# Order of the first chunks, the first weights and the crossbar transposes in a fused retention and Swish kernel

## The chip, the cores and the metric

The kernel runs on one core of one Trainium2 chip. The metric is the device time of one execution in microseconds; the median over several runs counts. A profile is of one single execution and has its own time.

## The reference, cut to what matters

```python
B, H, S, D = 8, 8, 576, 64                     # q, k, v: float32 [B, H, S, D]
scores = (1 / sqrt(D)) * (q @ k.transpose(0, 1, 3, 2))
gamma = 1 - 2 ** (-5 - arange(H))
Dmat = where(i >= j, gamma[h] ** (i - j), 0)   # causal decay, positions i and j
att = (scores * Dmat) @ v
x = att.transpose(0, 2, 1, 3).reshape(B * S, H * D)     # 4608 x 512
h = x @ w_in                                   # 512 x 2048
g = h * sigmoid(beta * h)                      # beta: one number for each of the 2048 columns
out = g @ w_out                                # 2048 x 512, float32
```

## The kernel before, in words

The decay is split into a factor of the query's position (`gq`, with the scale) and one of the key's position (`gv`, put on the values). What is left of the decay within a chunk is a mask of ones and zeros. The first 512 positions of each batch element are four **chunks** of 128; the last 64 positions of two batch elements together make a **tail** of 128 rows. In the list `seq` (lines 51 to 56) the chunks and tails are numbered in the order in which they are attended: 0 to 3 are batch 0, 4 to 7 batch 1, 8 to 11 batch 2, 12 to 15 batch 3, 16 the first tail, 17 to 20 batch 4, 21 a tail, 22 to 25 batch 5, 26 to 29 batch 6, 30 a tail, 31 to 34 batch 7, 35 the last tail. A state (keys by values, summed in PSUM) carries what a chunk hands on to the next.

A chunk's steps are these functions. `load_kv` (line 84) loads its keys and values on SyncE's queue in rows of 64 numbers (256 bytes). `pre` (248) scales and casts them on POOL into `kn` and `vn`. The keys are then transposed, for chunks 0 to 7 on TensorE through PSUM (`t_k`, 293), and later for two chunks at once by a crossbar DMA that ScalarE issues (`x_k`, 279, through `turn`, 273). The queries have the same two ways: `load_q`, `pre_q` (234), `t_q` (286) or `x_q` (276); a tail has `load_tail` and `x_tail` (283). `a_sc` (306) makes the scores in two PSUM tiles and masks them on VectorE into `R`; `a_st` (367) adds to the state, which ScalarE copies to SBUF; `a_cross` (321) is the part of the output that comes from the state; `a_O` (341) is the part within the chunk, and copies the transposed result into `xT`, the input of the second half.

The second half works on **blocks** of 512 rows (the four chunks of a batch element; block 8 holds the tails). `up` (387) multiplies by 128 columns of `w_in` in four matmuls, and ScalarE applies Swish from PSUM into `gT` (396); it can be given a part of the chunks (`c0`, `cn`). `down` (400) multiplies by four of the sixteen row groups of `w_out` and, at the last of them, copies the sum on VectorE into `ot` (414) and stores it from SyncE. Both use the PSUM tag `mm` with three buffers. The weights come as float32 pieces (`pieces`, 159; `load_w_in`, `load_w_out`) into four staging buffers, which the output also uses, and are cast to bf16 (`cast_w_in`, 173; `cast_w_out`, 187).

The order of the work is written by hand, and every engine runs its instructions in that order. Lines 438 to 466 are the start: queries of block 0, chunks 0, 1, 2, the first weights. From line 474 a list `fill` holds the calls of `up` and `down` in order, and `streams` holds the other steps, each with a number. `merged` (424) puts a step ahead of the fill item whose index is not below its number. `d0` is the index of block 0's first `down`, `u1` that of block 1's first `up`. Block 0's up is split: four products for chunks 0 to 2, then four for chunk 3 alone, then twelve whole ones; chunk 3 is attended among them (`steps(3, ...)`). From block 2 on, `group` (505) sets the steps of each chunk at distances ahead of the place `at` of its scores. `load_kv` has six buffers, `load_q` two, `kn` and its transpose three pairs, `vn` five. A SyncE load that waits for a buffer holds up what is queued behind it, and a crossbar transpose that ScalarE issues stands between its activations.

## Time and profile before

| what | value |
|---|---|
| median of 13 runs | 322.5 us (320.68 to 325.67) |
| the profiled execution: its time | 321.35 us |
| its span, first to last instruction | 319.6 us |
| TensorE matmuls busy | 302.5 us (95%) |
| ScalarE busy | 138.4 us |
| VectorE busy | 108.0 us |
| POOL busy | 96.0 us |
| moved by DMA | 53.82 MB |
| first up product of block 0 | 17.47 us |
| first down product of block 0 | 35.49 us |
| first up product of block 1 | 58.10 us |
| scores of chunk 8 (block 2) | 70.48 us |
| first up product of block 2 | 94.18 us |

All times within the execution count from the start of the span. A line of the timeline gives start, duration, engine, line, operation, what is written from what, the shape and the count; in brackets is the idle time of that engine just before and what ended it. PE is TensorE, ACT is ScalarE, DVE is VectorE, SPq and ACTq are the queues on which SyncE and ScalarE issue DMAs. Matmuls overlap, so the busy time of TensorE is more than its work.

### The profile page before, as it was taken

What the parts mean: (1) busy time and instruction counts of PE and PEld (TensorE: products, weight loads), DVE (VectorE), ACT (ScalarE), POOL (GpSimd) and SP (SyncE); (2) the same over time, 40 slices, a digit from 0 to 9 for tenths busy, and PEclk for the clock granted to TensorE, in tenths of its full rate; (3) what the DMA queues carried; (4) which work ended last, traced back from release to release, by engine and by line L of the source; (5) the groups of instructions that cost most, each with busy time, mean ns of one, the idle gap of its engine ahead of it and who ended that gap; (6) DMA issues with size and microseconds to landing.
All of it is one profiled execution on the core that took longest, in us unless ns stands there. A gap on an engine that the chain in (4) does not pass through costs nothing.

```text
span 319.6 us, 5205 instructions
## 1 busy us (share of the span) xinstructions
PE 302.5 (95%) x2078; PEld 153.0 (48%) x2113; DVE 108.0 (34%) x191; ACT 138.4 (43%) x241; POOL 96.0 (30%) x127
## 2 busy tenths in 40 slices
PE   7779988979999999999999999999799999999996
PEld 5545445434554445444444444444345444444444
DVE  6746456113560135224423343234324420010012
ACT  5567726654127601770067206720275117406700
POOL 2652075834530562174227120292220000000000
PEclk9799999999999999999999999999999999999999
DMA  8999999999979969995999736969841110032012
GB/s 208 259 345 386 372 208 269 248 207 204 229 198 157 238 139 225 231 198 128 229 246 157 161 102 129 250 102 225 215 39 33 68 66 0 2 79 53 2 59 72
DMA packets 127591, 53.82 MB, mean 168 GB/s; under 512 B 109888, under 2 KB 119504, under 8 KB 127568
## 3 DMA queue, kind: packets, MB, share of 16 engines
q1 hardware_dynamic: 97968, 46.15, 61.3%
q10 hardware_dynamic: 29600, 7.35, 14.5%
q8 instruction: 16, 0.26, 0.4%
q14 instruction: 7, 0.06, 0.1%
HBM read 36.71 MB, written 9.44 MB: 144 GB/s over the span
## 4 chain that ended last, share of the span: by engine, by line
PE 74%; DMA 13%; SPq 5%; POOL 3%; issue 2%; ACT 1%; DVE 1%; ACTq 0%; POOLq 0%; DVEq 0%
PE po L407 33%; PE ph L394 31%; DMA kT<-kn 9%; PE O L352 3%; PE sc L314 3%; SPq L91 2%; DMA kvn<-in_k_dram 2%; DMA wt<-in_moe_w_in_dram 2%; PE O L338 2%; PE st L377 2%; SPq L102 1%; SPq L80 1%; POOL qs L244 1%; ACT gT L396 1%; POOL kn L267 1%
## 5 line engine op out<-in xcount | busy, mean ns | idle before, releaser
L394 PE MATMUL ph<-xT,w_in_sb 128*128 128x512 bf16 (+2 forms) x577 | 127.6, 373 | 4.4 <-ACT gT L396 1.6
L407 PE MATMUL po<-w_out_sb,gT 128*128 128x512 bf16 (+2 forms) x588 | 126.6, 367 | 1.2 <-issue 0.3
L396 ACT ACTIVATE gT<-ph,beta_sb 128x512 bf16<-128x512 f32 (+2 forms) x148 | 98.8, 678 | 65.9 <-PE ph L394 64.7
L394 PEld LDWEIGHTS <-w_in_sb 128*128 128x128 bf16 x592 | 56.3, 98 | 68.0 <-issue 3.6
L407 PEld LDWEIGHTS <-gT 128*128 128x128 bf16 x608 | 57.1, 98 | 61.8
L319 DVE TENSOR_TENSOR R<-sc,causal 128x512 bf16<-128x512 f32 x72 | 46.3, 684 | 79.2 <-PE sc L314 79.1
L414 DVE COPY ot<-po 128x512 f32<-128x512 f32 (+2 forms) x38 | 25.2, 663 | 112.3 <-PE po L407 112.3
L244 POOL TENSOR_TENSOR qs<-qn,gq 128x512 bf16<-128x512 f32 x26 | 27.5, 1081 | 66.7 <-DMA qn<-in_q_dram 52.0
L268 POOL TENSOR_TENSOR vn<-kvn,gv 128x512 bf16<-128x512 f32 x32 | 33.3, 1042 | 14.4 <-DMA kvn<-in_v_dram 12.1
L382 ACT CAST sbd<-st 64x256 bf16<-64x256 f32 x48 | 17.6, 367 | 41.9 <-PE st L377 39.0
L267 POOL CAST kn<-kvn 128x512 bf16<-128x512 f32 x32 | 19.5, 609 | 41.8 <-DMA kvn<-in_k_dram 24.6
L382 ACT CAST end<-st 64x256 bf16<-64x256 f32 x16 | 5.9, 367 | 39.5 <-PE st L377 39.4
L365 DVE CAST xT<-O 128x512 bf16<-128x512 f32 x29 | 19.7, 680 | 2.9 <-PE O L352 2.0
L314 PE MATMUL sc<-qT,kT 64*128 64x128 bf16 x256 | 12.9, 221 | 4.9 <-DMA kT<-kn 2.7
L314 PEld LDWEIGHTS <-kT 64*128 64x128 bf16 x288 | 8.2, 95 | 18.6 <-issue 10.8
L352 PE MATMUL O<-R,vn 128*64 128x128 bf16 x288 | 15.3, 227 | 0.0
L377 PE MATMUL st<-vn,kn 128*128 128x128 bf16 x128 | 12.5, 220 | 0.2 <-POOL vn L268 0.2
L352 PEld LDWEIGHTS <-vn 128*64 128x64 bf16 x288 | 9.4, 110 | 4.2 <-issue 0.6
L338 PE MATMUL O<-qT,sbd 128*128 128x128 bf16 x96 | 9.7, 225 | 0.0
L377 PEld LDWEIGHTS <-kn 128*128 128x128 bf16 x128 | 8.5, 99 | 1.3 <-issue 0.2
L204 PE MATMUL ph<-warm 128*128 128x256 f32 (+1 forms) x16 | 6.3, 544 | 1.3 <-DVE warm L113 1.3
L194 DVE TENSOR_SCALAR w_out_sb<-wt,rbeta_sb 128x512 bf16<-128x512 f32 x12 | 5.1, 481 | 5.6 <-DMA wt<-in_moe_w_out_dram 5.6
(55 smaller groups left out, 76.6 us busy)
## 6 DMA issues: line engine op xcount, KB each, us to landing
qn<-in_q_dram SPq DMA_DIRECT2D x16, 512.0 KB, 5.7
kvn<-in_k_dram SPq DMA_DIRECT2D x32, 256.0 KB, 6.3
kvn<-in_v_dram SPq DMA_DIRECT2D x32, 256.0 KB, 5.9
out_dram<-ot SPq DMA_DIRECT2D x31, 256.0 KB, 3.2
wt<-in_moe_w_out_dram SPq DMA_DIRECT2D x4, 1024.0 KB, 9.3
wt<-in_moe_w_in_dram SPq DMA_DIRECT2D x3, 1024.0 KB, 9.6
out_dram<-ot SPq DMA_DIRECT2D x9, 128.0 KB, 2.4
tln<-in_q_dram SPq DMA_DIRECT2D x8, 128.0 KB, 3.8
```

The costliest lines, as they stand in the source:

```text
L244: e.tensor_tensor(batch[b]["qs"][:, cs, hs], q_tiles[b][:, hs, cs].rearrange("p h i d -> p i h d"), gq[:, cs, hs].unsqueeze(3).to_broadcas ...
L267: nc.gpsimd.tensor_copy(kn[:, c % 2], t[:, 0])
L268: nc.gpsimd.tensor_tensor(vn[:], t[:, 1], gains(gv, c), ALU.mult)
L314: nc.tensor.matmul(view(sc[j][:, p, :]), L["kT"][r, p, :], rhs, start=True, stop=True, skip_group_check=True)
L319: nc.vector.tensor_tensor(R[:, j], sc[j][:], m_b, ALU.mult)
L352: nc.tensor.matmul(O[j * D:(j + 1) * D, p, :], vn[:, 2 * p + j, :], R[:, j, p, :], start=p == 0 and not (early and crossed), stop=early or ...
L377: nc.tensor.matmul(st[:, p, :], heads(L["kn"], p), heads(L["vn"], p), start=(c == 0 and p == 0), stop=True, skip_group_check=True)
L382: nc.scalar.copy(s[r, :, j * D:(j + 1) * D], st[r, :, j * D:(j + 1) * D])
L394: nc.tensor.matmul(ph, w_in_sb[:, ko, fo * P:(fo + 1) * P], xts[m][:, ko, :, w], start=(ko == 0), stop=(ko == KO - 1))
L396: nc.scalar.activation(gts[m][:, fo, :, w], ph, ACT.Silu, scale=beta_sb[:, fo:fo + 1])
L407: nc.tensor.matmul(po[:, :nn], gT[:, fo, ms, :], w_out_sb[:, fo, n0:n0 + nn], start=(fo == 0), stop=(fo == FO - 1))
L414: nc.vector.tensor_copy(ot, po[:, :nn])
```

## The change

All four first chunks are loaded ahead of the weights, and chunk 3 is attended in the start like chunks 0 to 2; block 0's up is whole from its first product. The first two pieces of `w_in` become 256 and 256 columns, and their casts go to POOL and VectorE. For chunk 3 ScalarE copies one of the two score tiles to SBUF as bf16 (`half`), and VectorE masks it from there. In block 1, the first four products of up are made for chunks 4 to 6 and then for chunk 7 alone, and chunk 7 is attended among them. The loads of q(2) and of chunks 8 and 9 come right behind those of chunk 7, and chunks 10 and 11 have places of their own. In `group` the loads, the scaling steps and the crossbar transposes have larger distances ahead of the scores.

```diff
-    for n in range(CB - 1):
+    for n in range(CB):
         load_kv(n)
...
-    pieces = [(0, 384), (384, 128)] + [(f, 512) for f in range(512, d_ff, 512)]
+    pieces = [(0, 256), (256, 256)] + [(f, 512) for f in range(512, d_ff, 512)]
...
-    def cast_w_in(g):
-        t = wts.pop(g)
+    def cast_w_in(g, kos=range(KO)):
+        t = wts[g]
         f0, fn = pieces[g]
-        for ko in range(KO):
-            if g == 1 and ko < 2 or g == 0 and ko == 0:
-                nc.scalar.copy(w_in_sb[:, ko, f0:f0 + fn], t[:, ko])
-            else:
-                (nc.gpsimd if g < 2 or ko == KO - 1 else nc.vector).tensor_copy(w_in_sb[:, ko, f0:f0 + fn], t[:, ko])
+        for ko in kos:
+            on_pool = ko == KO - 1 or g == 0 and ko > 0 or g == 1 and ko > 1
+            (nc.gpsimd if on_pool else nc.vector).tensor_copy(w_in_sb[:, ko, f0:f0 + fn], t[:, ko])
...
     for g in range(NP):
-        if g == 1:
-            load_kv(CB - 1)
         load_w_in(g)
...
-        (nc.vector.tensor_copy if i == CB - 1 else nc.scalar.copy)(live[i]["kT"], T[:])
+        nc.scalar.copy(live[i]["kT"], T[:])
...
+        if i == CB - 1:
+
+            half = sb.tile([P, HP, P], BF16, name="half", tag="half", bufs=1)
+            nc.scalar.copy(half[:], sc[1][:])
+            sc[1] = half
         for j in range(2):
             nc.vector.tensor_tensor(R[:, j], sc[j][:], m_b, ALU.mult)
...
-            tag, bufs = ("mm", 3) if i == 1 else ("O", 1)
+            tag, bufs = ("mm", 3) if i in (1, 3) else ("O", 1)
...
-        if i == CB - 2:
+        if i == CB - 1:
             nc.vector.tensor_copy(x[:, :2], O[:, :2])
             nc.scalar.copy(x[:, 2:], O[:, 2:])
         else:
-            (nc.scalar.copy if i < E and i != CB - 1 else nc.vector.tensor_copy)(x, O[:])
+            (nc.scalar.copy if i < E else nc.vector.tensor_copy)(x, O[:])
...
     t_k(2)
     a_st(1)
-    cast_w_in(0)
     a_sc(2)
+    pre(3)
     a_O(1)
     warm_up(1, 128)
     a_cross(2, True)
+    t_k(3)
+    a_st(2)
+    cast_w_in(0, range(1, KO))
+    a_sc(3)
+    a_O(2)
+    a_cross(3, True)
+    a_st(3)
     warm_up(1, 128)
-    a_O(2)
-    a_st(2)
+    cast_w_in(0, range(1))
+    warm_up(1, 128)
+    a_O(3)
+    cast_w_in(1)
...
-    fill = [F(up, 0, fo, 0, CB - 1) for fo in range(4)] + [F(up, 0, fo, CB - 1, 1) for fo in range(4)]
-    fill += [F(up, 0, fo) for fo in range(4, FO)]
+    fill = [F(up, 0, fo) for fo in range(FO)]
     d0 = len(fill)
...
     u1 = len(fill)
-    fill += [F(up, 1, fo) for fo in range(FO)]
+    fill += [F(up, 1, fo, 0, CB - 1) for fo in range(4)] + [F(up, 1, fo, CB - 1, 1) for fo in range(4)]
+    fill += [F(up, 1, fo) for fo in range(4, FO)]
     fill += [F(down, 1, ms, f0) for ms in range(MB // P) for f0 in range(0, FO, 4)]
-    base = {1: u1}
+    base = {1: u1 + 4}
...
-    streams = [steps(3, 0, 1, 2, 3.5, 3.5, 3.5),
-               [(0.1, F(load_w_out, 0)), (2.5, F(cast_w_in, 1)), (6, F(cast_w_in, 2)), (6.2, F(load_w_out, 1)),
-                (10, F(cast_w_in, 3)), (10.1, F(load_w_out, 2)), (14, F(cast_w_in, 4)), (14.1, F(load_w_out, 3))],
-               [(d0 - 4 + 3.5 * g, F(cast_w_out, g)) for g in range(WG)],
-               [(14.2, F(load_q, 1))] + [(14.2, F(load_kv, n)) for n in range(CB, E)],
-               [(d0 + 7, F(pre_q, 1, n)) for n in range(4)] + [(d0 + 8.5, F(t_q, 1, 0)), (d0 + 9.8, F(t_q, 1, 1))],
-               steps(4, d0 + 7.5, d0 + 9.9, d0 + 10.7, d0 + 11.5, d0 + 11.6, d0 + 11.9),
-               steps(5, d0 + 9, d0 + 11.2, d0 + 11.8, d0 + 12.5, d0 + 12.6, d0 + 12.9),
-               steps(6, d0 + 10, d0 + 12.2, d0 + 12.8, d0 + 13.5, d0 + 13.6, d0 + 13.9),
-               steps(7, d0 + 11, d0 + 13.2, d0 + 13.8, d0 + 14.5, d0 + 14.6, d0 + 14.9)]
+    streams = [[(0, F(load_w_out, 0)), (2.1, F(cast_w_in, 2)), (2.2, F(load_w_out, 1)),
+                (6.1, F(cast_w_in, 3)), (6.2, F(load_w_out, 2)), (10.1, F(cast_w_in, 4)), (10.2, F(load_w_out, 3))],
+               [(d0 - 4 + 3.3 * g, F(cast_w_out, g)) for g in range(WG)],
+               [(10.3, F(load_q, 1))] + [(10.3, F(load_kv, n)) for n in range(CB, E)],
+               [(10.4, F(load_q, 2))] + [(10.4, F(load_kv, n)) for n in range(E, E + 2)],
+               [(d0 + 8.6, F(load_kv, E + 2)), (d0 + 10.1, F(load_kv, E + 3))],
+               [(d0 + 8, F(pre_q, 1, n)) for n in range(4)] + [(d0 + 9.6, F(t_q, 1, 0)), (d0 + 10.6, F(t_q, 1, 1))],
+               steps(4, d0 + 8.5, d0 + 11, d0 + 11.8, d0 + 12.7, d0 + 12.8, d0 + 12.9),
+               steps(5, d0 + 10, d0 + 11.9, d0 + 12.8, d0 + 13.7, d0 + 13.8, d0 + 13.9),
+               steps(6, d0 + 11, d0 + 12.95, d0 + 13.8, d0 + 14.7, d0 + 14.8, d0 + 14.9),
+               steps(7, d0 + 12, d0 + 15, u1 + 0.8, u1 + 2.7, u1 + 2.8, u1 + 2.9)]
...
-                st += [(at - 24, F(load_tail, c)), (at - 12, F(pre, i)), (at - 8, F(x_tail, i))]
+                st += [(at - 28, F(load_tail, c)), (at - 14, F(pre, i)), (at - 10, F(x_tail, i))]
...
                 if c == 0:
-                    xs, ps = ((8.5, 7), (14, 13, 12, 11)) if near else ((11, 9.5), (17, 16, 15, 14))
-                    st += [(at - 24, F(load_q, b))] + [(at - a, F(pre_q, b, x)) for x, a in enumerate(ps)]
+                    xs, ps = ((9, 7.5), (14, 13, 12, 11)) if near else ((14, 12.5), (20, 19, 18, 17))
+                    st += [(at - 32, F(load_q, b))] if not near else []
+                    st += [(at - a, F(pre_q, b, x)) for x, a in enumerate(ps)]
                     st += [(at - a, F(x_q, b, x)) for x, a in enumerate(xs)]
                 if c % 2 == 0:
-                    p0, p1, x0 = (13, 12, 8.5) if c else (9, 8.5, 5.5) if near else (13, 12, 7.5)
-                    st += [(at - 23, F(load_kv, n)), (at - 22.5, F(load_kv, n + 1)), (at - p0, F(pre, i)),
-                           (at - p1, F(pre, i + 1)), (at - x0, F(x_k, b, c // 2))]
+                    p0, p1, x0 = (9, 8.5, 6) if near and c == 0 else (16, 15, 10.5)
+                    if not near:
+                        st += [(at - 29, F(load_kv, n)), (at - 26, F(load_kv, n + 1))]
+                    st += [(at - p0, F(pre, i)), (at - p1, F(pre, i + 1)), (at - x0, F(x_k, b, c // 2))]
```

## The prediction, made before the changed kernel ran

> **What bounds the kernel now.** I read the page first (busy shares, slices, chain), then the waits of TensorE, then the timeline of each engine where TensorE waits, then the DMA issues one by one. The page says that TensorE sets the time, with the chain on it for 74%, and that the DMA engines are full for the first third.
>
> ```profile
> PE 302.5 (95%) x2078; PEld 153.0 (48%) x2113; DVE 108.0 (34%) x191; ACT 138.4 (43%) x241; POOL 96.0 (30%) x127
> DMA  8999999999979969995999736969841110032012
> PE 74%; DMA 13%; SPq 5%; POOL 3%; issue 2%; ACT 1%; DVE 1%; ACTq 0%; POOLq 0%; DVEq 0%
> ```
>
> A 512-column matmul goes through every 0.216 us: a product of up or down (four of them) is 0.863 us. So only TensorE's idle pieces can be won, and these are few; its waits and its timeline give them (start, duration, then idle before in brackets):
>
> ```profile
> 17.47 0.81 PE L394 MATMUL ph<-xT,w_in_sb 128*128 128x384 bf16 x4 [0.28 <-DVE xT L362]
> 18.57 0.40 PE L296 MATMUL T<-ident,kn 128*128 128x128 bf16 x4 [0.30 <-POOL kn L267]
> 21.57 0.86 PE L394 MATMUL ph<-xT,w_in_sb 128*128 128x384 bf16 x4 [0.86 <-ACT w_in_sb L178]
> 24.03 0.38 PE L394 MATMUL ph<-xT,w_in_sb 128*128 128x128 bf16 x4 [0.80 <-DVE xT L365]
> ...
> 45.57 0.61 PE L290 MATMUL T<-ident,qs 128*128 128x128 bf16 x8 [0.84 <-DVE ot L414]
> 49.46 0.40 PE L314 MATMUL sc<-qT,kT 64*128 64x128 bf16 x8 [0.46 <-ACT kT L297]
> ...
> 66.00 1.89 PE L394 MATMUL ph<-xT,w_in_sb 128*128 128x512 bf16 x8 [0.84 <-ACT gT L396]
> 68.67 1.89 PE L394 MATMUL ph<-xT,w_in_sb 128*128 128x512 bf16 x7 [0.77 <-ACT gT L396]
> ...
> 80.10 0.40 PE L314 MATMUL sc<-qT,kT 64*128 64x128 bf16 x8 [0.34 <-DMA kT<-kn]
> ...
> 227.06 0.40 PE L314 MATMUL sc<-qT,kT 64*128 64x128 bf16 x8 [2.33 <-DMA kT<-kn]
> ```
>
> The reader should see four places: block 0's start (17.5 to 24.0), block 1's attention (43 to 58), ScalarE held up in block 1's up (65 to 69), and one late transpose at 227. Everything else is TensorE at its pace. The third place is explained by ScalarE's timeline: it issues the crossbar transposes itself, and the activation behind them comes late.
>
> ```profile
> 63.27 1.95 ACTq L274 DMA_TRANSPOSE qT<-qs  x1
> 65.27 0.69 ACT L396 ACTIVATE gT<-ph,beta_sb 128x512 bf16<-128x512 f32 x1 [1.39 <-PE ph L394]
> 65.39 2.48 ACTq L274 DMA_TRANSPOSE kT<-kn  x1
> 65.85 0.68 ACT L396 ACTIVATE gT<-ph,beta_sb 128x512 bf16<-128x512 f32 x1
> 67.92 2.49 ACT L396 ACTIVATE gT<-ph,beta_sb 128x512 bf16<-128x512 f32 x4 [1.39 <-PE ph L394]
> ```
>
> **What the Trainium skill says.** (1) "DMA: Bandwidth & Descriptors", section "Issuing engines are not separate DMA queues": transfers of all issuers run on the same 16 engines and interleave. The trace agrees: transposes land in 3.1 to 3.4 us where SyncE loads nothing (114 to 118, 142 to 152, 176 to 180 us) and in 4.6 to 9.4 us beside loads. (2) "Perfetto Trace Analysis", section "DMA Instruction — HWDGE (DVE, Sync)": the profiled window of an issue holds the wait for the shared descriptor generator and its use. The ACTq rows are such windows, 1.25 to 2.81 us for a transpose, and ScalarE computes nothing behind one. (3) "VectorE: DVE Perf Modes", section "The perf-mode tier table": tensor_tensor on bf16 in SBUF runs at twice the rate of one with a PSUM operand. No row of before shows it.
>
> **Part 1, all four first chunks ahead of the weights.** SyncE's order becomes q, chunks 0 to 3, then w_in as 256+256 columns instead of 384, chunk 3, 128. POOL's products on the values of chunks 0, 1, 2 started as these landed, at 9.02, 11.36 and 13.65, 2.3 us a chunk, so chunk 3's keys come near 14.8 and its values near 16.0. The first weights: 0.75 MB took 2.15 us after chunk 2, so 0.5 MB takes 1.4 us: 17.5; the second 0.5 MB by 19 to 20.5. The whole volume ahead of the third piece is unchanged, so that one lands at 23.0 as before, or about 1.4 us earlier if wider rows go faster.
>
> Chunk 3's path on ScalarE, in program order, each by its row: x(1) copied by 16.1; kT copy 0.59 (to 16.9, after its transposes at 16.0); state copies of chunk 2, 0.76 (17.65); the new copy of half the scores, priced at 0.59 like a 128x512 copy (18.25); x(2) 0.59 (18.85); state copies 0.75 (19.6); half of x(3) 0.37 (20.0). On VectorE the mask of the SBUF half costs an estimated 0.37 (0.684 times the page's ratio), at least 0.35, at most 0.68; it lies beside x(2)'s copy, so it costs nothing, and if that cover goes, 0.3. So the first up starts at 20.0 instead of 17.47, but then runs whole: 16 x 0.863 = 13.8, to 33.8. Now down starts at 35.49. **Gain 1.7.** ScalarE's casts of weights (0.51 and 0.49) go to POOL and VectorE and are hidden there, as is one more warm-up product (0.37) while TensorE waits for x(3): POOL's three of 256 columns are about 0.35 each after 17.5; pieces 3 to 5 (23.0, 25.7, 28.4 before, cast within 1.5) are needed at 23.5, 26.9 and 30.4, so weights cap the gain soon after. w_out's casts start at 31.1, 33.8, 36.5 and 39.3 and end 1.5 to 2 later; they are needed at 33.8, 36.4, 39.0 and 41.6, 0.8 or more after. Bounds: 0.5 if chunk 3 comes 1.2 later, 2.3 if weights come early.
>
> **Part 2, block 1.** SyncE's loads of q(1) and chunks 4 to 7 are back to back already (30.4 to 47.7), and POOL waits for them; so POOL's kn copies of chunks 4 to 7 (43.98, 45.77, 48.12, 50.42) stay where they are while TensorE comes 1.7 us earlier. The wait of 0.84 goes, since t_q's second PSUM buffer is now asked for one down after it is given up; the six pieces from 43 to 58 (0.84, 0.46, 0.23, 0.23, 0.16, 0.16) sum to 2.1. New waits, walking the order: second t_q for its scaled queries (44.03) 0.3; t_k(4) 0.15, t_k(5) 0.3, t_k(6) 0.35 for kn. Chunk 7 moves into up. There its state copies (0.75) and x copy (0.59) queue on ScalarE behind activations, and the four one-chunk products wait about 0.5 for x(7); 128-column products in place of a quarter of a 512 cost 0.25 more together (in block 0: 16 matmuls in about 1.1 where 0.86 is ideal). That is 1.85 against 2.1: **gain 0.25**, bounds -1.0 to 1.2. The first up of block 1 begins near 53.7 (now 58.1), but with chunk 7 inside it.
>
> **Part 3, block 2's transposes.** Every issue counts for ScalarE. From 54.4 it has to do, up to the activation of up(1,11): four activations of 384 columns (0.58), four of 128 (0.30), eight of 512 (0.69) = 9.0; chunk 7's copies 1.34; and three transposes, at 1.33 + 1.95 + 2.48 = 5.76 as now. Together 16.1, against 11.7 of TensorE's. ScalarE is the bound of this stage: up(1,11) ends near 69.1 with the buffers in between, where it ends at 70.4 now. The scores of chunk 8 follow there, and need the keys' transpose. Its data cannot come much sooner: q(2) and chunks 8, 9 stand right behind chunk 7 on SyncE in both orders, and POOL finishes chunk 9's keys at 61.0. It is issued at about 63.3 (now 65.39), and lands after 4.6 us as now, or 7.2 as beside loads: new is that SyncE puts q(3) and chunks 12, 13 in front of it (steps 33, 36, 39; now 41 to 43). That gives 67.9 to 70.5; I take 69.5, so of the 1.95 won so far **0.95 is given back**, bounds a gain of 1.0 and a loss of 2.5. Chunks 10 and 11 are loaded ahead of output stores (chunk 10's load waits for chunk 4's slot, free at 45.7, and two stores queue behind it; SyncE comes there near 55, so nobody waits), so the wait of 0.34 at 80.1 goes: **0.3**.
>
> **Part 4, transposes issued further ahead in later blocks.** The late one at 227 is x_k(7,0): issue 219.82, landing 7.2 us later, behind three others since 213.35, all beside the loads of block 7's last two chunks. From the first issue to the need it has 11 fill steps and one attention group (about 1.3), 10.8 us, and takes 13.7. Now the queries' turn is put 14 steps ahead instead of 11 and the keys' 10.5 instead of 7.5; with two groups between that is 14.7 us. So the 2.33 goes, if POOL is in time: its queries waited for q(7) until 205.84, and that load moves 8 steps ahead, past the tail's six loads. **Gain 2.0**, bounds 0 and 2.33. The price: the first transposes of blocks 4 and 5 now run alone, and after the change a block's last two chunks are loaded beside them (for block 5 at steps 118 and 121, with x_q at 118 and x_k at 122). Landing then rises from 3.3 toward 7; margin is 14.7 - 13.7 = 1.0. I take **0.2 lost**, bounds 0 and 2. The tail of the program keeps its order.
>
> **Sum.** 1.7 + 0.25 - 0.95 + 0.3 + 2.0 - 0.2 = 3.1 us. The profiled execution took 321.35 (span 319.6, the rest lies around it), so 318.2 for one like it; it is 1.15 under the median 322.5 of the runs shown, so the median goes to 319.4. A difference of 0.5% (1.6 us) is about what a measurement of this kernel can tell from no change.
>
> **Rivals.** A, as summed: 319.4, chance 0.46. B, transposes issue fast: at the 1.33 of the first instead of 5.76 for three, ScalarE has 1.8 less; Part 3 then gives nothing back, Part 2 reaches its better half: 3.1 + 1.8 + 0.9 = 5.8, 316.7; chance 0.20. For it speaks that most transposes issue in 1.25 to 1.35, against it that three in a row did not. C, the gain is lost to arrival: chunks 4 to 9 land where they land, TensorE waits at chunk 8's scores until the old 70.5, and only Part 4 is kept in half: 1.0, 321.5; chance 0.19. D, slower: loads put ahead make the transposes late. If keys land 9.4 us after issue (as at 70.65) instead of 4.6 to 7, chunk 8 is late by 3 more than in A, and blocks 4, 5, 7 miss their margin of 1.0 by 0.9 each: 319.4 + 3 + 2.7 = 325.1; it decides once transposes beside loads take over 8 us. For it the full DMA row speaks, against it that of 28 only one took over 8; chance 0.15.
>
> Faster: A and B, 0.66; same: C, 0.19; slower: D, 0.15. The range 316.5 to 323.0 leaves out D and the best of B. A's own range is 318 to 320.9.
>
> **What would show it.** First full up near 20.0 and down near 33.8 (Part 1); no idle before t_q, but short waits for kn and for x(7) (Part 2); chunk 8's scores near 69.5, with the transposes' issue windows between activations (Part 3); no wait of over 0.5 at block 7's keys (Part 4). I am wrong if chunk 3 is turned later than 17, if ScalarE's transposes cluster more tightly than now, or if a new wait on kT of over 1 us stands in blocks 3 to 6.

## The result, and the profile after

| | kernel before | changed kernel |
|---|---|---|
| median | 322.27 us (48 runs, 319.49 to 325.67) | 326.8 us (11 runs, 323.37 to 329.29) |
| ratio to before, 95% interval | 1 | 1.0126 (1.0092 to 1.0161) |
| profiled execution: time, span | 321.35, 319.6 us | 324.02, 322.3 us |
| first down of block 0 | 35.49 us | 34.23 us |
| scores of chunk 8 | 70.48 us | 73.05 us |
| scores of chunk 10 | 80.10 us | 85.23 us |

The changed kernel is slower, by about 1%; 319.4 was predicted, with a range up to 323.0. Measured once more (10 runs) it took 325.79 us against 322.67, ratio 1.0061 (1.0008 to 1.0113). Its runs scatter over almost 2%, and the ratios leave out executions more than 1.5% above the fastest, so that a ratio can be smaller than that of two medians.

The page of the changed kernel, in the same rows as before and with the row of TensorE's clock:

```profile
PE 305.0 (95%) x2080; PEld 153.5 (48%) x2115; DVE 108.2 (34%) x192; ACT 139.2 (43%) x241; POOL 96.5 (30%) x127
PEclk9799999979999999999999999999999999999999
PE 83%; DMA 8%; SPq 4%; issue 1%; ACT 1%; POOL 1%; DVE 0%; ACTq 0%; POOLq 0%
```

TensorE's busy time rose by 2.5 us for nearly the same work, and the clock row has a 7 in the ninth slice (64 to 73 us), where the kernel before has 9. Loss and gain are in TensorE's timeline:

```profile
19.42 3.63 PE L395 MATMUL ph<-xT,w_in_sb 128*128 128x512 bf16 x15 [0.52 <-DVE xT L363]
...
58.41 4.81 PE L395 MATMUL ph<-xT,w_in_sb 128*128 128x128 bf16 x31 [0.36 <-ACT xT L366]
64.62 1.02 PE L395 MATMUL ph<-xT,w_in_sb 128*128 128x512 bf16 x4 [1.41 <-ACT gT L397]
68.68 4.44 PE L395 MATMUL ph<-xT,w_in_sb 128*128 128x512 bf16 x12 [3.03 <-ACT gT L397]
84.05 1.25 PE L408 MATMUL po<-w_out_sb,gT 128*128 128x512 bf16 x5 [2.80 <-ACT gT L397]
85.23 0.40 PE L310 MATMUL sc<-qT,kT 64*128 64x128 bf16 x8
```

The start is as predicted, and the wait of 2.33 at 227 us is gone (chunk 31's scores are at 229.69 with no idle ahead). But between 58 and 95 us the waits sum to 7.60 us, where before they sum to 0.84 + 0.77 + 0.34 = 1.95. Three of the four are for an activation of ScalarE. What held ScalarE shows in its own timeline (rows of the DMA issues and of the activation behind one):

```profile
59.37 1.49 ACTq L270 DMA_TRANSPOSE qT<-qs  x1
...
61.02 2.82 ACTq L270 DMA_TRANSPOSE qT<-qs  x1
...
63.96 3.93 ACTq L270 DMA_TRANSPOSE kT<-kn  x1
67.94 1.85 ACT L397 ACTIVATE gT<-ph,beta_sb 128x512 bf16<-128x512 f32 x3 [3.37 <-issue]
```

That is the cluster of block 2's transposes. The issues took 1.49 + 2.82 + 3.93 = 8.24 us against 5.76 before. The wait at 84 us, from here on **the gate**, has another source. The chain of waits that leads to it, in order of time:

```profile
63.96 6.84 DMA kT<-kn
70.80 0.02 issue
70.82 0.39 SPq L80
...
71.26 8.52 DMA qn<-in_q_dram
...
79.94 2.05 POOL qs L240 x2
...
82.01 1.25 ACTq L270
...
83.31 0.70 ACT gT L397
...
84.05 1.25 PE po L408 x5
```

Read from the end: down product 12 of block 1 waits for block 1's last activation. In front of that activation, in ScalarE's queue, stands block 3's first query transpose. It waits for POOL to scale q(3), the queries of block 3; POOL waits for q(3)'s load, and SyncE issues that load only at 70.82, at the moment when block 2's first key transpose has landed (63.96 + 6.84 = 70.80). In the kernel before, the same transpose stands behind block 1's last activation and holds no activation, though its data comes no earlier than 78 us there either:

```profile
78.19 3.87 ACTq L274 DMA_TRANSPOSE qT<-qs  x2
```

Why does a load of queries wait for a transpose of keys? SyncE's timeline of the changed kernel shows the gap:

```profile
60.35 0.61 SPq L91 DMA_DIRECT2D kvn<-in_k_dram  x1
67.41 0.39 SPq L91 DMA_DIRECT2D kvn<-in_v_dram  x1
67.90 1.01 SPq L418 DMA_DIRECT2D out_dram<-ot  x2
70.82 1.00 SPq L80 DMA_DIRECT2D qn<-in_q_dram  x2
```

The compiled program's lists of waits, cut here to four rows and with what each moves, give the reason. In this program the transfers of SyncE and ScalarE take eight semaphores (counters that tell of a landing; DMAHW0 to 7) in turn, and each transfer first waits for the landing of the last user of its semaphore:

```
ACT  DmaTransposeAnt qT<-qs   [waits DMAHW4_49,Pool_49]    block 2's first query transpose
SP   DMACopy kvn<-in_v_dram   [waits DMAHW4_49]            chunk 11's values
ACT  DmaTransposeAnt kT<-kn   [waits DMAHW0_49,Pool_49]    block 2's first key transpose
SP   DMACopy qn<-in_q_dram    [waits DMAHW0_49]            q(3)
```

So chunk 11's values go out when that query transpose has landed (59.37 + 8.0 = 67.37, issue at 67.41), and q(3) when the key transpose has. The kernel before shows the same elsewhere: its store at 68.54 follows the landing of its first query transpose at 61.81 + 6.7 = 68.51.

TensorE's clock in two stretches of the changed kernel (window, its length, then busy time of PE, PEld, DVE, ACT, POOL; the third figure from the end is the granted clock):

```profile
68.68:73.05 4.37, 4.37 (x13) 1.47 (x13) 0.00 (x0) 2.48 (x4) 1.27 (x2) 0.61 1.30 250
81.25:84.05 2.80, 0.00 (x0) 0.00 (x1) 0.00 (x0) 0.74 (x2) 2.80 (x4) 1.00 1.39 218
```

After the idle 3.03 us the clock was at half for 3.4 us, and 12 matmuls took 4.44 us, where 12 x 0.216 = 2.6 is their pace.

### The profile page after: what moved, and what is told of

It is laid out like the page before. It is cut to its first block, busy times and chain, and to the rows that moved or that the text cites. A ratio compares the mean times of both kernels' runs of the same rounds, so it can differ in the third digit from the quotient of the medians.

```text
span 322.3 us, 5213 instructions
## 1 busy us (share of the span) xinstructions
PE 305.0 (95%) x2080; PEld 153.5 (48%) x2115; DVE 108.2 (34%) x192; ACT 139.2 (43%) x241; POOL 96.5 (30%) x127
## 3 DMA queue, kind: packets, MB, share of 16 engines
q10 hardware_dynamic: 29600, 7.35, 14.9%
## 4 chain that ended last, share of the span: by engine, by line
PE 83%; DMA 8%; SPq 4%; issue 1%; ACT 1%; POOL 1%; DVE 0%; ACTq 0%; POOLq 0%
PE po L408 37%; PE ph L395 35%; PE sc L310 3%; PE O L353 3%; SPq L91 3%; DMA wt<-in_moe_w_in_dram 3%; DMA qn<-in_q_dram 3%; DMA kT<-kn 2%; PE st L378 2%; PE O L339 2%; POOL qs L240 1%; SPq L170 1%; PE O L336 0%; SPq L80 0%; ACT gT L397 0%
## 5 line engine op out<-in xcount | busy, mean ns | idle before, releaser
L395 PE MATMUL ph<-xT,w_in_sb 128*128 128x512 bf16 (+2 forms) x575 | 129.4, 377 | 6.8 <-ACT gT L397 4.4
L366 DVE CAST xT<-O 128x512 bf16<-128x512 f32 x28 | 19.0, 680 | 0.9 <-PE O L336 0.9
L178 DVE CAST w_in_sb<-wt 128x512 bf16<-128x512 f32 (+1 forms) x12 | 5.7, 523 | 5.2 <-DMA wt<-in_moe_w_in_dram 5.2
```

What stands on the lines that cost most here:

```text
L395: nc.tensor.matmul(ph, w_in_sb[:, ko, fo * P:(fo + 1) * P], xts[m][:, ko, :, w], start=(ko == 0), stop=(ko == KO - 1))
```

## The experiments

Edits are against the changed kernel where nothing else is said. "Waits" are TensorE's idle pieces of 0.25 us or more between 58 and 95 us in the profiled execution, "clock" is what a granted clock under 1 cost between 58 and 100 us (1 minus clock, summed over the time). A profile is of one execution; the ratio compares runs on one chip, where the kernel before took 321.52 to 322.67 us.

| kernel | waits | clock | profiled execution | median | ratio to before (95%) |
|---|---|---|---|---|---|
| before | 1.95 | 0 | 321.35 | 322.27 | 1 |
| changed | 7.60 | 1.71 | 324.02 | 326.8 | 1.0126 (1.0092 to 1.0161) |
| changed, measured again | 5.10 | 3.41 | 322.61 | 325.79 | 1.0061 (1.0008 to 1.0113) |
| queries of block 3 at the old distance | 8.06 | 3.42 | 326.5 | 325.17 | 1.0102 (1.0022 to 1.0181) |
| block 2 on TensorE | 0.35 | 0 | 318.94 | 318.29 | 0.9892 (0.9804 to 0.998) |
| transposes issued from SyncE | 14.17 | 8.53 | 331.23 | 330.07 | 1.0234 (1.0135 to 1.0333) |
| Parts 1 and 2 alone | 3.82 | 0 | 320.7 | 320.96 | 0.9979 (0.9951 to 1.0006) |
| q(3) loaded early | 5.93 | 3.42 | 323.4 | 321.78 | 1.0014 (0.9984 to 1.0043) |
| before, with Part 4 alone | 2.19 | 0 | 322.1 | 321.26 | 0.9983 (0.9949 to 1.0017) |
| block 2's turns as before | 6.24 | 3.41 | 325.21 | 325.13 | 1.0103 (1.0018 to 1.0188) |
| block 2 on TensorE, four warm-ups out | 1.34 | 0 | 318.23 | 318.38 | 0.9912 (0.9877 to 0.9948) |
| the same, q(3) loaded early | 0.35 | 0 | 317.21 | 317.59 | 0.9895 (0.9833 to 0.9956) |
| before, query transposes of block 3 ahead | 3.12 | 0 | 321.25 | 322.53 | 1.0032 (1.0004 to 1.0061) |
| both undone | 7.47 | 1.71 | 323.12 | 322.57 | 1.0017 (0.9987 to 1.0047) |
| loads in order of need | 8.25 | 3.41 | 325.19 | 322.38 | 1.0027 (1.0002 to 1.0052) |
| waits filled | 4.14 | 0 | 323.76 | 323.29 | 1.0045 (1.0015 to 1.0075) |

My first theory was that the cluster's waits and the one at 84 us add up, each with its own cause: 2.8 us for the place of block 3's query transposes, the rest for the cluster. The rivals were that the loads put ahead make every transfer late, and that ScalarE, which issues the transposes, is what holds TensorE.

**Block 3's query transposes at the old distance** (11 and 9.5 steps ahead).

```diff
-    ... else ((14, 12.5), (20, 19, 18, 17))
+    ... else ((11, 9.5) if b == 3 else (14, 12.5), (20, 19, 18, 17))
```

> The changed kernel with one edit: block 3's two query transposes go back to 11 and 9.5 steps ahead (behind block 1's last activation) instead of 14 and 12.5. Theory (two holds of ScalarE: 4.4 us at the cluster of block 2's transposes, 2.8 us where block 3's query transpose waits for its data ahead of block 1's last activation): the 2.8 us wait of down near 84 us goes, the 4.4 us near 64 to 69 stay; the time falls by about 2.5 us, to some 324.3. Rival (loads put ahead make all transposes late): no change within 0.5 us. Rival (the granted clock falls after idle pieces): falls by 2.5 us and a little more.

Measured 325.17 us, ratio 1.0102. The wait near 84 us went, and a longer one came in its place:

```profile
90.71 0.61 PE L339 MATMUL O<-qT,sbd 128*128 128x128 bf16 x4 [5.63 <-ACT sbd L383]
```

The next transpose in ScalarE's queue, that of block 3's first keys, waited for chunk 13's keys and was issued only at 87.23, with the state copies behind it. POOL cast those keys at 86.59, without a pause since it began to scale q(3) at 81.04, and q(3) itself had landed only 11.3 us after its second issue; so the late q(3) stands behind this wait as well. The theory of two separate waits with 2.8 us to win fell: with the query transposes moved alone, the wait goes to the next transpose whose data is late.

**Block 2 transposed on TensorE**, so that its four crossbar transposes are gone; VectorE copies the results.

```diff
-    st += [(at - a, F(x_q, b, x)) for x, a in enumerate(xs)]
+    st += [(at - a, F(t_q if near else x_q, b, x)) for x, a in enumerate((5, 4) if near else xs)]
...
-    st += [(at - p0, F(pre, i)), (at - p1, F(pre, i + 1)), (at - x0, F(x_k, b, c // 2))]
+    st += [(at - p0, F(pre, i)), (at - p1, F(pre, i + 1))]
+    st += [(at - 3, F(t_k, i)), (at - 2, F(t_k, i + 1))] if near else [(at - x0, F(x_k, b, c // 2))]
...
-        nc.scalar.copy(live[i]["kT"], T[:])
+        (nc.scalar.copy if i < E else nc.vector.tensor_copy)(live[i]["kT"], T[:])
```

> The changed kernel with block 2's queries and keys transposed on TensorE and copied by VectorE, so that ScalarE issues no crossbar transpose before block 3. It adds 32 TensorE transposes (about 1.8 us at 55 ns) . Theory: the 4.4 us at 64 to 69 go, and q(3) is no longer held behind the keys' transpose, so that most of the 2.8 us near 84 goes too: 4.4 + 2.5 - 1.8 = 5 us less than the changed kernel, some 321.8, with the clock at 1.0 throughout. Rival (ScalarE is full there anyway): at most 2 us less. Rival (arrival of chunks 8 and 9 limits): TensorE waits for kn or for the queries near 62 to 66.

Measured 318.29 us, ratio 0.9892. No wait over 0.35 us is left in the stretch, chunk 8's scores come at 69.75 and chunk 10's at 79.40, although this profile began at half clock (down at 35.99 instead of 34.23). So the loss is tied to block 2's four transposes, and the rest of the change is a gain. The edit takes away their issues on ScalarE, their DMA traffic and their places among the semaphores together, so it does not tell these apart.

**All crossbar transposes issued from SyncE.**

```diff
-        nc.scalar.dma_start_transpose(...)
+        nc.sync.dma_start_transpose(...)
```

> The changed kernel with all 28 crossbar transposes issued by SyncE instead of ScalarE. Theory: no transpose stands between activations, so both waits on activations (4.4 and 2.8 us) go and the time falls by up to 7 us, to 320, less what later loads cost now that SyncE waits for POOL ahead of a transpose. Rival (transposes land late because loads stand beside them): waits on the transposed keys and queries appear in place of those on activations and the time falls by less than 3 us.

Measured 330.07 us, ratio 1.0234. TensorE no longer waits for activations there, but 13.82 us for the keys of chunk 8: block 2's first query transpose was issued only at 70.19, behind loads in SyncE's queue that wait for semaphores of their own. ScalarE's hold is thus removed as a cause of waits and replaced by a worse one; issuing from SyncE is no way out.

**Parts 1 and 2 alone**: the start and block 1 of the change, with `group` and the loads of block 2 of the kernel before.

```diff
-               [(10.4, F(load_q, 2))] + [(10.4, F(load_kv, n)) for n in range(E, E + 2)],
-               [(d0 + 8.6, F(load_kv, E + 2)), (d0 + 10.1, F(load_kv, E + 3))],
...
-                    xs, ps = ((9, 7.5), (14, 13, 12, 11)) if near else ((14, 12.5), (20, 19, 18, 17))
+                    xs, ps = ((8.5, 7), (14, 13, 12, 11)) if near else ((11, 9.5), (17, 16, 15, 14))
...
-                    p0, p1, x0 = (9, 8.5, 6) if near and c == 0 else (16, 15, 10.5)
+                    p0, p1, x0 = (13, 12, 8.5) if c else (9, 8.5, 5.5) if near else (13, 12, 7.5)
```

> The changed kernel with the distances and the loads of block 2 on as before: only the first chunks, the first weights and block 1's parts are changed. Theory: the start keeps its gain (down of block 0 at 34.2, not 35.5; block 1's fifth product near 59.9, not 61.6), block 2's transposes cost ScalarE 5.8 to 7 us instead of 8.2, block 3's query transpose is back behind block 1's last activation, and the late transpose near 227 is back: about the time of before, 321 to 323. Rival (the early start itself, by its clock or its loads, is what costs): 325 or more.

Measured 320.96 us, ratio 0.9979, so 0.7 us of the 2.0 that the two parts win by 60 us is left, and the interval does not exclude none. The cluster took 1.12 + 1.74 on TensorE, a key transpose was late by 0.61 at 89.63, and the one at 226 us was back with 1.62.

**q(3) loaded early**: only the load of block 3's queries moved, ahead of chunk 10's loads.

```diff
-    st += [(at - 32, F(load_q, b))] if not near else []
+    st += [(d0 + 8.5 if b == 3 else at - 32, F(load_q, b))] if not near else []
```

> The changed kernel with q(3) loaded right behind chunks 8 and 9 (ahead of chunk 10) instead of behind chunk 11 and the stores. Theory (q(3) is late because its load takes over a DMA semaphore from block 2's key transpose and must wait until that has landed): q(3) is there by about 66, so the 2.8 us wait of down near 84 goes or shrinks below 1; the cluster's 4.4 us stay: 324 to 325. Rival (any step of block 3 is late since the DMA engines are full): a wait of 2 us or more stays near 84, only with another tensor, and chunks 10 and 11 come later.

Measured 321.78 us, ratio 1.0014. q(3) was issued at 56.36 instead of 70.82, block 3's first query transpose at 78.64 instead of 82.01, and the gate was gone. One load's place is worth 0.5 to 1.1% by the ratios (1.0061 or 1.0126 against 1.0014). The cluster cost 2.56 here, and a wait stands in a new place:

```profile
75.28 4.44 PE L395 MATMUL ph<-xT,w_in_sb 128*128 128x512 bf16 x12 [3.02 <-ACT gT L397]
```

It is for activations behind block 2's second key transpose, issued only at 72.48, since chunk 11's keys went out at 67.69, after two stores whose window lasts from 60.10 to 67.60. So chunk 10's scores came at 84.97, hardly sooner than the 85.23 of the changed kernel: in the profiled executions another wait took the gate's place, and they do not show where the gain of the ratio lies.

**Part 4 alone**, in the kernel before: the larger distances for the tails and for blocks 4 to 7 only.

```diff
+                    if b > 3:
+                        xs, ps = (14, 12.5), (20, 19, 18, 17)
...
+                    if b > 3:
+                        p0, p1, x0, l0, l1 = 16, 15, 10.5, 29, 26
```

> The kernel before with only the larger distances of loads, scaling steps and transposes for the tails and for blocks 4 on. Theory: the wait of 2.3 us near 227 goes and nothing else moves: 1.5 to 2.3 us less than before. Rival (loads beside transposes make these late): the same or slower.

Measured 321.26 us, ratio 0.9983, not told from no change. The late transpose at 227 us is gone in the profile; this execution had two others (1.64 at 81.91 and 1.34 at 106.13), for key transposes that landed 10.8 and 8.1 us after their issue, as the rival says.

**Block 2's transposes at the distances of the kernel before.**

```diff
-    xs, ps = ((9, 7.5), ...
+    xs, ps = ((8.5, 7), ...
...
-    p0, p1, x0 = (9, 8.5, 6) if near and c == 0 else (16, 15, 10.5)
+    p0, p1, x0 = (9, 8.5, 5.5) if near and c == 0 else (16, 15, 10.5)
```

> The changed kernel with block 2's first three transposes at the distances of before (8.5, 7 and 5.5 steps ahead, not 9, 7.5 and 6), with nothing else changed. Theory A (the order among the activations lengthens the wait: with one activation instead of two between the second and the third transpose, the third issue holds ScalarE from the landing of the first): the waits near 62 to 69 fall from 4.4 to about 2, q(3) comes earlier, 3 to 5 us less than the changed kernel. Theory B (the windows are long because chunks 10 and 11 are loaded in front of them): the waits stay at 3.5 to 4.5.

Measured 325.13 us, ratio 1.0103, no better than the changed kernel. Yet the cluster was short (issue windows 1.33, 1.47, 1.25), it cost TensorE 0.32, and chunk 8's scores came at 68.73, 4.3 us sooner. By chunk 10's scores (84.75) nearly all of it was lost at the gate:

```profile
82.50 2.31 PE L408 MATMUL po<-w_out_sb,gT 128*128 128x512 bf16 x5 [5.57 <-ACT gT L397]
```

q(3) was issued at 68.03, scaled from 78.39, its transpose issued at 80.47. What the cluster saves, TensorE waits at the gate, so in this version the gate decides and the cluster's length does not. This is the theory that I took on from here; the version above, which has no gate and a new wait, already says that it is not the whole.

**Block 2 on TensorE, four warm-ups out**: the second version above without four of the start's warm-up products.

```diff
-    warm_up(1, 128)
```

> The changed kernel with block 2 transposed on TensorE (as in e2_block2_on_tensor), and without the four warm-up products between the first chunks. Theory (with the clock granted at half speed from 11 to 20 us TensorE itself is the chain of the start, and the warm-ups stand on it with 0.8 + 1.2 us): block 0's first up starts 1.5 to 2 us earlier than 22.2 where the clock is low, about 1 us less in the median. Rival (they keep the clock up): the low clock lasts longer, and the first up starts no earlier.

Measured 318.38 us, ratio 0.9912, the same as with them. Down began at 34.52 with a start at half clock (35.99 with them), and the gate came back with 0.99 at 77.91.

**The same, with q(3) loaded early.**

```diff
-    st += [(at - 32, F(load_q, b))] if not near else []
+    st += [(d0 + 8.5 if b == 3 else at - 32, F(load_q, b))] if not near else []
```

> The changed kernel with block 2's queries and keys transposed on TensorE, without the four warm-ups, and with block 3's queries loaded one cluster earlier. Theory (the query transpose of block 3 ahead of block 1's last activation holds ScalarE until those queries are there): the wait of 0.99 near 78 us that was left goes, no wait on an activation over 0.4 us between 60 and 85 us, time 317.0 to 317.8, about 1 us under the version with the late load (318.4). Rival (only the cluster of transposes costs, and it is gone already): same as 318.4 within 0.3.

Measured 317.59 us, ratio 0.9895. The 0.99 is gone (q(3) is scaled from 70.94), and TensorE has no wait over 0.35 us from 21 us to the end. This is the best version, 1.05% under the kernel before; it is not told from the two before it by time.

**The kernel before, with block 3's query transposes ahead**: the suspected cost by itself.

```diff
+                    if b == 3:
+                        xs = (14, 12.5)
```

> The kernel before with one thing moved: block 3's two query transposes at 14 and 12.5 steps ahead of their use, so that the first stands ahead of block 1's last activation on ScalarE. Theory: it waits for queries that are scaled near 78 us, the activation is held to about 80, the down products of block 1 wait 1.5 to 2.5 us for it, time 323.4 to 324.8. Rival (the cluster of block 2 alone makes the changed kernel late): no change, 321.9 to 322.4.

Measured 322.53 us, ratio 1.0032 (1.0004 to 1.0061), 1.0 us. The mechanism is as stated: the transpose was issued at 78.08, the last activation came at 79.38 after ScalarE had been idle for 4.86 us, and the down products waited 1.23 at 80.12:

```profile
80.12 1.25 PE L407 MATMUL po<-w_out_sb,gT 128*128 128x512 bf16 x5 [1.23 <-ACT gT L396]
```

The wait is under what I expected (1.5 to 2.5) and under the changed kernel's 2.80, although TensorE comes to it 2.4 us sooner (78.89 against 81.25): q(3) is scaled from 76.01 here and from 79.94 there.

**Both undone**: block 2's transposes as before and q(3) loaded early.

```diff
-    xs, ps = ((9, 7.5), ...
+    xs, ps = ((8.5, 7), ...
...
-    st += [(at - 32, F(load_q, b))] if not near else []
+    st += [(d0 + 8.5 if b == 3 else at - 32, F(load_q, b))] if not near else []
...
-    p0, p1, x0 = (9, 8.5, 6) if near and c == 0 else (16, 15, 10.5)
+    p0, p1, x0 = (9, 8.5, 5.5) if near and c == 0 else (16, 15, 10.5)
```

> The changed kernel with block 2's transposes at the distances of the kernel before and block 3's queries loaded one cluster earlier: both suspected waits taken away together, all other parts of the change kept. Theory: neither the 1.4 and 3.0 us of the cluster nor the 2.8 near 84 us stays, waits on activations between 60 and 85 us sum to under 1.2 us, chunk 10's scores by 80.5, time 318.5 to 320.5. Rival (the full DMA engines make the transposes late whatever their place): 321.8 or more.

Measured 322.57 us, ratio 1.0017: a miss, the rival's number. The gate is gone, but there are waits of 2.73 and 4.39. SyncE's timeline says why for the second:

```profile
58.52 1.04 SPq L91 DMA_DIRECT2D kvn<-in_v_dram  x1
59.66 7.03 SPq L418 DMA_DIRECT2D out_dram<-ot  x2
66.78 0.45 SPq L91 DMA_DIRECT2D kvn<-in_k_dram  x1
```

With q(3)'s two transfers ahead, an output store became the one that shares a semaphore with block 2's first query transpose (landing at 59.74 + 6.5 = 66.2, the window of the two stores ends at 66.7). Chunk 11's keys, behind it, were issued at 66.78 (at 60.31 in the version with block 2's turns as before), cast at 71.44, their transpose was issued at 72.08, and the activation behind it came at 74.42. The version with q(3) loaded early has the same order of transfers, and its wait of 3.02 is this one. Ahead of the 2.73 stands the second query transpose, with an issue window of 3.88; why it is long here and 1.47 in the version with block 2's turns as before, at the same distances, is not shown.

```profile
65.86 3.61 PE L395 MATMUL ph<-xT,w_in_sb 128*128 128x512 bf16 x16 [2.73 <-ACT gT L397]
75.16 4.29 PE L395 MATMUL ph<-xT,w_in_sb 128*128 128x512 bf16 x12 [4.39 <-ACT gT L397]
```

**Loads in order of need**: the version with both undone, with chunk 11 directly behind chunk 10 and q(3) behind it, ahead of the stores.

```diff
-               [(d0 + 8.6, F(load_kv, E + 2)), (d0 + 10.1, F(load_kv, E + 3))],
+               [(d0 + 8.6, F(load_kv, E + 2)), (d0 + 8.7, F(load_kv, E + 3))],
...
-    (d0 + 8.5 if b == 3 else at - 32, F(load_q, b))
+    (d0 + 8.75 if b == 3 else at - 32, F(load_q, b))
```

> The version with both undone, whose waits stayed (2.7 and 4.4 us), with one thing changed: chunk 11's loads stand directly behind chunk 10's and block 3's queries behind them, ahead of the two output stores of that time, so that none of these loads is the eighth transfer behind block 2's first query transpose (it then is a store that waits for its landing). Theory (keys of chunk 11 were issued only at that landing, 66.8, cast at 71.4, their transpose at 72.1, and ScalarE held behind it): chunk 11's keys issued by 62, cast by 68, the second key transpose issued by 69, waits on activations between 60 and 85 us under 1.5 us in sum, time 318.5 to 320.5. Rival (the full DMA engines delay the transfers whatever the order): the waits stay over 5 us, time 321.8 or more.

Measured 322.38 us, ratio 1.0027: again a miss in time. Chunk 11's keys were issued at 60.34 and cast at 68.41, and their transpose went out at 69.05, as I expected. But in that profile block 2's first key transpose, issued at 64.42 amid the loads of chunks 10 and 11 and q(3) (2 MB issued between 58 and 67 us), needed 10.6 us to land:

```profile
75.12 0.60 PE L310 MATMUL sc<-qT,kT 64*128 64x128 bf16 x8 [6.18 <-DMA kT<-kn]
```

Here the rival's mechanism is seen: with the loads early, the transposes land late. This execution lies 2.8 us over its median, so the 6.18 is probably at the long end.

**Waits filled**: two groups of ten matmuls of 512 columns that nobody reads, ahead of up product 9 of block 1 and ahead of down product 12.

```diff
+    def spin(n):
+        T = psum.tile([P, MB], F32, name="T", tag="T", bufs=1)
+        for _ in range(n):
+            nc.tensor.matmul(T[:], w_in_sb[:, 0, :P], w_in_sb[:, 0, :MB], ...)
...
+    streams = [[(u1 + 13, F(spin, 10)), (u1 + 23, F(spin, 10))],
```

> The changed kernel with 2 x 10 matmuls of 512 columns whose result nobody uses, ahead of block 1's up product 9 (where it waits 3.03 us) and ahead of down product 12 (2.80 us): 2.16 us of TensorE each, inside the waits. Theory (a wait costs itself and, after it, half-clock windows of 1.71 us each): the half clock at 69 to 72 us goes, the scores of chunk 10 come 1 to 2 us earlier than 85.2, and the median falls by 1.5 to 3 us against the changed kernel on the same chip. Rival (the waits alone make the loss): no gain, 0 to 1 us slower since the added products reach past shorter waits.

Measured 323.29 us, ratio 1.0045, against 325.79 and 1.0061 for the changed kernel on the same chip (2.5 us by the medians, 0.5 us by the ratios, whose intervals overlap: the gain in time is not settled). The mean granted clock rose from 0.978 to 0.987, about what the kernel before had (0.985), and no half clock is left between 58 and 100 us. But chunk 10's scores came at 84.64, not 1 to 2 us before 85.2:

```profile
68.38 2.75 PE L401 MATMUL ph<-xT,w_in_sb 128*128 128x512 bf16 x12 [0.50 <-ACT gT L403]
...
83.46 1.25 PE L414 MATMUL po<-w_out_sb,gT 128*128 128x512 bf16 x5 [2.04 <-ACT gT L403]
```

12 matmuls take 2.75 us at full clock (4.44 before), and TensorE then waits 2.04 us more at the gate, on top of the ten filling matmuls (2.3). The slow clock ahead of the gate is thus hidden by the gate.

**The changed kernel again**, beside it.

> The changed kernel as it is, beside the one with filled waits on the same chip, with a second profile. Theory: ratio to the kernel before 1.009 to 1.016 as measured, mean granted clock 0.979, the gate ahead of down product 12 between 2.5 and 6 us, and more half-clock windows between 60 and 95 us than the one of the first profile. Rival (the excess of the median lies elsewhere): the same waits and clock there as in the first profile, and a new wait in another place.

Measured 325.79 us, ratio 1.0061. Its profile is of a shorter execution (322.61): waits of 1.38, 2.45 and only 0.92 at 82.65, but two half-clock windows (67 to 73 us, 12 matmuls took 5.28). q(3) was issued at the same 70.82, landed 7.1 us after its second issue instead of 8.5 and was scaled from 78.54, 1.4 us earlier than in the first profile; chunk 10's scores came 1.4 us earlier, at 83.84. My expectation of a gate between 2.5 and 6 us was wrong: what is steady is when the gate opens. In five of the six profiles with this wait, down product 12 goes 4.11 or 4.12 us after POOL begins to scale q(3): 79.94 and 84.05, 78.54 and 82.65, with filled waits 79.34 and 83.46, with block 2's turns as before 78.39 and 82.50, in the kernel before with the query transposes ahead 76.01 and 80.12, whether TensorE came early or late. In the sixth, with four warm-ups out, it is 4.27 (73.64 and 77.91).

## Why the prediction was wrong, point by point

- **Part 1 was right.** First full up at 19.42 (predicted 20.0), down at 34.23 (33.8): 1.26 gained where 1.7 was said. Chunk 3's keys were cast at 14.82 (14.8). The mask of the half that ScalarE copied took 0.52 us (0.43 and 0.45 in two other profiles) beside 0.69 for the half in PSUM, so 1.3 to 1.6 times as fast and not twice, the ratio behind the estimate of 0.37; it lay beside x(2)'s copy, as said.
- **Part 2 was right in its direction and too low.** Block 1's first up at 53.95 (53.7); the wait for x(7) was 0.36 (0.5). The waits for the new keys, counted at 1.1 together with that for the queries, did not come: no other piece between 42 and 58 us is over 0.1. By the fifth product of block 1, at 59.51 against 61.55, the changed kernel is 2.0 us ahead, so 0.8 came from here (0.25).
- **Part 3 failed.** "Of the 1.95 won so far 0.95 is given back, bounds a gain of 1.0 and a loss of 2.5": from 2.0 ahead at 59.5 us it went to 5.13 behind at chunk 10's scores, a loss of 7.2. The sum from the profile: waits after 59.5 us of 1.41 + 3.03 + 2.80 = 7.24 less 1.95 before, and about 1.7 for the half clock, 7.0. Two terms are behind it. First, "three transposes, at 1.33 + 1.95 + 2.48 = 5.76 as now" were 8.24, so the cluster was mis-sized; the mechanism was right, and chunk 8's scores came at 73.05 instead of 69.5. Second, the count of what ScalarE has to do ended at block 1's product 11. It left out, and so put at nothing, that the larger distances set **block 3's** first query transpose ahead of block 1's last activation. By itself, in the kernel before, that costs a wait of 1.23 us and about 1.0 us of time. In the changed kernel q(3) comes 3.9 us later than there (scaled from 79.94 against 76.01). The prediction counted that q(3)'s load stands ahead of later loads, and took it for a load that comes earlier; it was issued 1.65 us later (70.82 against 69.17), since its turn fell on the semaphore of a transpose still under way, and then took 2.3 us longer to land (8.5 against 6.2 for the second half).
- **The 0.3 at 80.1** went, as said, but was of no use behind the gate.
- **Part 4 was right in the profile.** The 2.33 is gone, no wait on keys stands in blocks 3 to 6, and from 5.13 behind at chunk 10 the changed kernel comes to 2.7 behind at the end. In the runs, Part 4 alone gave 0.9983 (0.9949 to 1.0017), not told from nothing and less than the 2.0 us that were forecast for it.
- **The rivals.** D had nearly the right time (325.1) by "loads put ahead make the transposes late". The parts of it that sum to its time, late keys for chunk 8 and misses in blocks 4, 5 and 7, were not there in the changed kernel's profile, so that its time was met by luck. The loss came from ScalarE's queue order and from loads that wait for transposes, the other way round. But transfers that slow each other down have a part in it: with block 2's turns as before, q(3) was issued sooner than in the kernel before (68.03 against 68.95) and yet scaled 2.3 us later (78.39 against 76.11).
- **The range** reached to 323.0 since I gave the case beyond 0.15, from one transpose of 28 over 8 us. That counted how often such a landing occurs, not that a place in the program's order can make one certain to be waited for.

What stays open: without the gate, versions that keep block 2 on the crossbar end at 1.0014 to 1.0027, though Parts 1, 2 and 4 (1.26 + 0.8 + 2.4 us by the milestones above) should bring them to some 317.8. Each moved the wait to another transfer, and only taking the four transposes away ended it. Whether the share of DMA time (14.9% of the engines for 28 transposes, so 0.149 x 322.3 / 28 = 1.7 us of all engines each) or the shared semaphores weigh more in that remainder was not taken apart. It is shown that the loss goes with block 2's four transposes, and that block 3's query transpose ahead of an activation costs time by itself. How the loss divides between the cluster, the gate and late landings is not shown. Nor is it settled how much of the scatter of the changed kernel's runs is clock: its first profile is 2.8 us under its median, and only the 2.7 us between the profiled executions are accounted for here, not the 4.5 between the medians.

## What to carry to other kernels

Before a DMA issue is moved ahead in an engine's queue, list what then stands behind it and when its data can be there at the earliest: a transpose that waits for its input holds every activation behind it, and the same step one place later held no activation here. Look at landings and not only at issues: q(3), issued 0.9 us sooner, was there 2.3 us later. A gain ahead of such a gate is only waited away, so look first for the chain that opens it. Where queues share a ring of semaphores, each load put in or moved shifts which later transfer waits for which; look up the pairs in the compiled order, not only in the queue's own.

## What the runs showed of the hardware that was not expected

- **The clock after a wait.** The Trainium skill, "TensorE: Matmul & The Clock Gate", section "What's actually happening", says that TensorE falls to half its clock after an idle window of about 3.4 us and comes back after a busy one, the windows running freely. The traces agree on the size: what the clock cost between 58 and 100 us was 0, 1.71 or 3.41 us in all versions but one, so one or two windows of 3.4 us at 0.50, and 8.53 (five) with the 13.82 us wait. They differ on what is enough. With a grid of 3.41 us laid through each profile's own half-clock windows, the clock fell nine times between 40 and 300 us in the 16 profiles, and each time TensorE had been idle for 2.03 to 3.41 us of the window before; after windows with 1.82 us or less it never fell. So some 60% of a window was enough, and what counts is how waits lie in the windows: the 2.80 us wait that ended at 84.05 lay over two of them with 1.31 and 1.49 us, and the clock stayed, while in the second profile parts of two waits (1.38 and 2.45) made 2.39 in one window.
- **Half clock in the start.** In seven of the 16 profiles TensorE ran at 0.50 for 10.24 us, beginning 8.9 to 11.4 us after the start of the span, in spite of short products in that time: it cost 5.12 us of clock there, against 1.71 in seven others. With the changed start, block 0's down then came at 35.16 to 35.99 instead of 34.23; without four of the warm-ups it came at 34.52 even so.
- **Landing of one crossbar transpose**: 3.0 to 10.8 us for the same 128 x 8 x 128 numbers over all profiles; in the kernel before it took 3.1 to 3.4 us where SyncE loaded nothing beside it.
